# Four weight loads move from SyncE's queue to ScalarE's queue

## Chip, cores and metric

The kernel runs on one core of a Trainium2 chip. The metric is the device time of one launch in microseconds, the median of several runs. "Load" here means a DMA transfer from device memory (HBM) into SBUF; an engine's "queue" is the instruction stream from which a DMA is issued.

## What is computed

The reference chains three parts: attention with a window, a mixture of four experts that all tokens pass through, and a second mixture of eight experts in which each token is assigned to one.

```python
scores = scale * q @ k.T + bias            # B=2, H=8, S=768, D=64; 96 local keys and 8 global ones
a = softmax(where(keep, scores, -1e9));  x = (a @ v) as [1536, 512]
p = domain_probs / domain_probs.sum(-1)    # [1536, 4]
for e in range(4):
    x1 += p[:, e:e+1] * (relu(x @ w1[e]) @ w2[e])          # w1[e] 512x1024, w2[e] 1024x512
logits = x1 @ w_gate                       # greedy assignment by logit, 192 tokens for each of 8 experts
out[mask_e] = relu(x1[mask_e] @ v1[e]) @ v2[e]
```

## The kernel before

Every matrix product of the experts is done in float16 with a high and a low part, so that it keeps float32's accuracy. A weight matrix therefore goes through a small chain of its own before it can be used. One matrix (2 MB) is a *job* `k`; jobs 0 and 1 are the two matrices `w1[0]` and `w2[0]` of the first expert. Each job is loaded in two halves `f` of 1 MB, as 128 partitions of four rows of 2 KB. The steps are named as follows; a suffix `.k` is the job (none for job 0), and a digit the half or the quarter:

- `wl0`, `wl1` (`w_fetch`, L501 to L510; the DMA is on L507): the load of a half into a slot. The first four loads, `wl0`, `wl1`, `wl0.1`, `wl1.1`, go to two slots in the tile `y` and two in the tile `xT`. The next expert's loads, `wl0.2` to `wl1.3`, use the same four slots, and each waits for the lows that read the half before it.
- `wsq0`, `wsq1` (`w_norm`, L459): 16 small TensorE matmuls for each half that build a Gram matrix in PSUM, whose diagonal is the sum of squares.
- `wsum` (L463, L465): VectorE reads the Gram matrix against the identity (`gramj`), and one TensorE matmul adds over partitions. `wsc` (L330 to L335): VectorE makes a power of two from it, the scale `wsr`.
- `whi0` to `whi3` (L580 on ScalarE, L582 on GpSimd): the scaled high part of a quarter. `wlo0` to `wlo3` (L524): the low part, on VectorE, 1.3 us each.

The first phase interleaves these steps with the attention, which takes the 1536 rows as 12 tiles of 128. For a tile j: `load.j` and `loadv.j` (L592) load k, q and v; `sq` (L599, ScalarE) their squares; `total`, `scale` a power of two each; `hi`, `lo` (L580/L582, L648) their two parts; `T0`, `T1` the turned q and k (for tile 0 by TensorE and copies on ScalarE, L669, and VectorE, L667); `swap` a second turned q; `diag` a scaled identity; `qk`, `max`, `exp`, `ph`, `pl`, `PT`, `pv`, `x` the attention itself; `slope` prepares the bias (L386, L387). `gate` loads and squares the router's matrix.

The order in which all these steps are put into the program is written out by hand in the string `ORDER1`, and each engine runs its own instructions in that order. Its start, with the four loads in it, reads:

```python
    slope3 load sq1 sq0 gate0 loadv slope7 gate1 gate2 sq2 slope6 slope2 total wl0 scale hi1/G wsq0 hi0 hi2 lo0 slope4
    lo1 wl1 slope1 lo2 diag/A T0 T1 wsq1 wl0.1 slope0 wsum wsc swap wl1.1 qk0 whi3/G max0 qk1 load.1 whi0 max1 wsq0.1
    whi1/G wsq1.1 exp0 wlo3 wlo1 whi2 slope5 wsum.1 wlo0 loadv.1 ph0/G sq1.1 load.2 exp1 sq0.1 wlo2 wl0.2 sq2.1 wsc.1
```

All loads of this phase are issued by SyncE (SP). SP computes nothing, so that there a load's place in the order matters only against other DMAs. ScalarE computes `sq`, half of the `hi` steps, copies from PSUM and the exponentials.

Of the kernel before, what the change touches and what calls it, by code (L numbers as in the profile page):

```python
# [298 lines left out]
class Net:  # L299
# [201 lines left out]
    def w_fetch(s, k, f, slot):  # L501

        (m, e), i = s.jobs[k]
        w = s.w[m][i]
        src = w[e, :, 512 * f:512 * f + 512] if i == 0 else w[e, 512 * f:512 * f + 512, :]
        r = slot()
        s.nc.sync.dma_start(r, src.rearrange("(k p) f -> p k f", p=128))  # L507
        s.raws[k, f] = (r, None)
        s.when[k, f] = 0
        s.nload = max(s.nload, 2 * k + f + 1)  # L510
# [1371 lines left out]
```

## Time and profile before

| | us |
|---|---|
| median of 3 runs | 863.86 |
| lowest, highest | 862.59, 866.21 |
| the profiled execution's own time | 861.97 |
| its span from first to last instruction | 860.2 |
| TensorE busy (matmuls) | 777.3 (90%) |
| VectorE busy | 608.4 (71%) |
| ScalarE busy | 502.2 (58%) |
| GpSimd busy | 206.4 (24%) |

Busy time is a mean over stages that have different limits, so the rows below are of single stretches. In rows, PE is TensorE, PEld its weight loads, DVE VectorE, ACT ScalarE, POOL GpSimd, SP SyncE; a q behind a name (SPq, ACTq) is the engine's sequencer, which issues DMAs and semaphore instructions.

### The profile page before, as it was taken

How to read it: one execution, taken by the hardware profiler on the slowest of the kernel's cores; microseconds unless marked ns; L12 is line 12 of the kernel's file. 1: busy time of each engine (PE TensorE's matmuls, PEld its weight loads, DVE VectorE, ACT ScalarE, POOL GpSimd, SP SyncE). 2: the span in 40 equal slices, each digit the busy share in tenths (PEclk: the TensorE clock that was granted, in tenths of full speed). 3: DMA queues.
4: the chain of work that ended last, by engine and by line, in shares of the span. 5: the costliest groups of instructions: out<-in, count | busy, mean ns of one | idle time of the engine just before them, and what ended most of it. 6: DMA issues, size and time to landing. Idle time of an engine off the chain costs nothing. (4 is left out here: it accounts for less than half of the span.)

```text
span 860.2 us, 21736 instructions
## 1 busy us (share of the span) xinstructions
PE 777.3 (90%) x8916; PEld 600.1 (70%) x8920; DVE 608.4 (71%) x1467; ACT 502.2 (58%) x1004; POOL 206.4 (24%) x238
## 2 busy tenths in 40 slices
PE   3688999999999999999999999979998757999996
PEld 3477767777777767678888887534443357888996
DVE  5998888777763644547879999986674625797890
ACT  5887786745352323334557979631056417989852
POOL 3553352332442224240210112000000022222221
PEclk9689999999999999999999999989999869999999
DMA  8996769664447311691333320249014279899811
GB/s 272 265 191 140 130 154 171 120 136 88 99 73 207 104 51 51 125 178 31 75 71 69 77 59 26 63 103 330 34 32 140 76 237 332 253 265 335 174 38 38
DMA packets 219652, 116.38 MB, mean 135 GB/s; under 512 B 187424, under 2 KB 187424, under 8 KB 219552
## 3 DMA queue, kind: packets, MB, share of 16 engines
q1 hardware_dynamic: 217504, 108.64, 50.6%
q0 software_dynamic: 2048, 6.34, 3.1%
q8 instruction: 70, 1.15, 0.6%
q14 instruction: 30, 0.25, 0.1%
HBM read 69.30 MB, written 12.63 MB: 95 GB/s over the span
## 5 line engine op out<-in xcount | busy, mean ns | idle before, releaser
L886 PEld LDWEIGHTS <-w 128*128 128x128 f16 x3456 | 248.1, 98 | 37.9 <-issue 4.1
L886 PE MATMUL pH<-xT,w 128*128 128x128 f16 (+1 forms) x3168 | 252.9, 235 | 2.2 <-ACT H L860 1.6
L1072 PE MATMUL pY<-w,xT 128*128 128x512 f16 x384 | 120.7, 386 | 4.6 <-DVE y L1086 4.6
L897 PE MATMUL pY<-w,hh 128*128 128x512 f16 x384 | 114.7, 381 | 0.0
L1033 ACT ACTIVATE Cj<-C 128x256 bf16<-128x256 bf16 (+11 forms) x88 | 75.3, 855 | 28.2 <-DVE C L1024 21.6
L1305 PEld LDWEIGHTS <-w 128*128 128x128 f16 x768 | 66.4, 101 | 28.5 <-DMA xg<-g 16.2
L1072 PE MATMUL pY<-w,hl 128*128 128x512 f16 x192 | 74.1, 386 | 0.0
L897 PE MATMUL pY<-w,hl 128*128 128x512 f16 x192 | 73.1, 381 | 0.0
L860 ACT ACTIVATE H<-pH 128x512 f32<-128x512 f32 (+1 forms) x70 | 38.4, 554 | 55.1 <-PE pH L886 34.4
L1305 PE MATMUL pH<-xg,w 128*128 128x192 f16 x528 | 51.5, 259 | 19.5 <-DMA xg<-g 17.0
L1072 PEld LDWEIGHTS <-xT 128*128 128x128 f16 x384 | 36.5, 99 | 42.1 <-issue 8.6
L1325 PE MATMUL pR<-hh,w 128*128 128x192 f16 x512 | 64.9, 246 | 0.0
L1325 PEld LDWEIGHTS <-w 128*128 128x128 f16 x768 | 63.3, 98 | 2.0 <-issue 1.9
L1325 PE MATMUL pR<-hl,w 128*128 128x192 f16 x256 | 63.0, 246 | 0.0
L1022 DVE TENSOR_SCALAR C<-w,Lg 128x1024 bf16<-128x1024 f32 (+7 forms) x98 | 58.8, 615 | 0.6 <-PE pw L1039 0.4
L762 ACT ACTIVATE t<-pS,mx,ec 128x256 f32<-128x256 f32 (+1 forms) x96 | 51.6, 541 | 2.2
L777 POOL TENSOR_TENSOR pp<-t,pp 128x512 f16<-128x512 f32 (+1 forms) x34 | 40.1, 1183 | 44.4 <-ACT pp L580 35.9
L494 DVE SCALAR_TENSOR_TENSOR w<-w,wsr,w 128x1024 f16<-128x1024 f32 x32 | 40.4, 1279 | 10.0 <-ACT w L580 9.9
L584 DVE TENSOR_SCALAR hh<-H 128x384 f16<-128x384 f32 (+1 forms) x53 | 20.9, 396 | 37.5 <-ACT H L860 37.0
L897 PEld LDWEIGHTS <-hh 128*128 128x128 f16 x384 | 32.9, 98 | 19.6
L1452 POOL TENSOR_TENSOR hl<-H,hh 128x512 f16<-128x512 f32 x26 | 32.9, 1265 | 56.3 <-DVE hh L584 31.7
L469 ACT ACTIVATE junk<-w 128x2048 f16<-128x2048 f32 x16 | 30.5, 1906 | 25.4 <-DMA w<-in_moe_w_dram 25.4
(298 smaller groups left out, 1537.7 us busy)
## 6 DMA issues: line engine op xcount, KB each, us to landing
w<-in_moe_w_dram SPq DMA_DIRECT2D x16, 1024.0 KB, 13.0
raw<-in_moe_w_dram SPq DMA_DIRECT2D x16, 1024.0 KB, 7.8
hl<-in_moe_w_dram SPq DMA_DIRECT2D x8, 1024.0 KB, 5.5
y<-in_moe_w_dram SPq DMA_DIRECT2D x4, 1024.0 KB, 6.7
xT<-in_moe_w_dram SPq DMA_DIRECT2D x4, 1024.0 KB, 11.5
rows<-xs SPq DMA_DIRECT2D x12, 260.0 KB, 2.1
x<-in_k_dram SPq DMA_DIRECT2D x12, 256.0 KB, 3.3
x<-in_q_dram SPq DMA_DIRECT2D x12, 256.0 KB, 3.9
```

The source lines that it names most:

```text
L494: V.scalar_tensor_tensor(l, r[:, d2], sc, h, op0=OP.mult, op1=OP.subtract)
L762: s.nc.scalar.activation(t[:, hh], ps[:, hh], AF.Exp, bias=mx[:, 1, hh:hh + 1], scale=e[:, 0:1], accum_out=s.SU[j][:, 2 * g + hh:2 * g + h ...
L777: (G if eng == "G" else V).tensor_sub(pl[:, x], t, ph[:, x])
L860: s.nc.scalar.activation(H, ps, AF.Relu, scale=HS)
L886: nc.tensor.matmul(o[f], w[:, d, 128 * (f0 + f):128 * (f0 + f) + 128], x[:, :, c], start=(d == 0 and i == 0), stop=(d == 3 and i == 2))
L897: nc.tensor.matmul(py, l[:, f], w[:, f], start=(f == 0 and i == 0), stop=(f == 7 and i == 2))
L1022: V.tensor_scalar(C[:, 8 * i:8 * i + n], x[:, :n, e], l, None, op0=OP.is_ge)
L1033: s.nc.scalar.activation(x, C, AF.Copy, accum_out=s.AC[j][:, 1, e:e + 1])
L1072: nc.tensor.matmul(py, a[:, f], w[:, f], start=(n == 0), stop=(n == 23))
L1305: nc.tensor.matmul(ps[0][:, f % 2], w[:, d, 128 * f:128 * f + 128], xg[:, :, c], start=(k == 0), stop=(k == 11))
L1325: nc.tensor.matmul(ps[0][:, d % 2], w[:, f, 128 * d:128 * d + 128], h[:, f], start=(k == 0), stop=(k == 23))
L1452: (nc.gpsimd if eng == "G" else nc.vector).tensor_sub(x[1], P.pop((e, j, c)), x[0])
```

## The change

`w_fetch` issues the DMA on ScalarE's queue for jobs 0 and 1, and on SP's queue for all others as before. The place of the four steps in `ORDER1` stays, and so do their slots and sizes.

```diff
@@ -504,7 +504,7 @@
         w = s.w[m][i]
         src = w[e, :, 512 * f:512 * f + 512] if i == 0 else w[e, 512 * f:512 * f + 512, :]
         r = slot()
-        s.nc.sync.dma_start(r, src.rearrange("(k p) f -> p k f", p=128))
+        (s.nc.scalar if k < 2 else s.nc.sync).dma_start(r, src.rearrange("(k p) f -> p k f", p=128))
         s.raws[k, f] = (r, None)
         s.when[k, f] = 0
         s.nload = max(s.nload, 2 * k + f + 1)
```

## Rows read from the trace of the kernel before

**Rows 1.** Busy time by stretches: stretch, length, PE, PEld, DVE, ACT, POOL, clock, DMA share, GB/s

```profile
0.00:80.00 80.00, 53.10 (x677) 44.27 (x678) 67.29 (x170) 61.26 (x155) 36.50 (x45) 0.85 0.87 221
80.00:300.00 220.00, 216.09 (x2779) 163.12 (x2783) 155.42 (x337) 123.18 (x312) 74.50 (x78) 0.99 0.61 130
```

**Rows 2.** The same view, of two stretches of the start-up

```profile
16.00:24.00 8.00, 3.96 (x67) 3.15 (x64) 7.29 (x15) 6.73 (x18) 6.34 (x5) 0.99 0.85 205
...
24.00:40.00 16.00, 10.07 (x82) 8.02 (x83) 15.17 (x40) 13.51 (x33) 7.30 (x9) 0.50 0.96 264
```

**Rows 3.** The same view, of the first transfers

```profile
2.00:6.00 4.00, 0.00 (x0) 0.00 (x0) 2.18 (x11) 1.60 (x6) 1.11 (x4) 1.00 1.06 213
6.00:16.00 10.00, 4.51 (x49) 4.00 (x49) 4.65 (x13) 5.64 (x17) 2.10 (x4) 1.00 1.03 383
```

**Rows 4.** Timeline of SP's queue: start, duration of the issue, what

```profile
3.35 1.33 SPq L507 DMA_DIRECT2D y<-in_moe_w_dram  x2
4.72 1.50 SPq L507 DMA_DIRECT2D xT<-in_moe_w_dram  x2
...
8.25 7.32 SPq L592 DMA_DIRECT2D x<-in_q_dram  x1
...
23.53 1.88 SPq L507 DMA_DIRECT2D y<-in_moe_w_dram  x2
```

**Rows 5.** Timeline of TensorE: the Gram matmuls, with the idle time before

```profile
10.88 1.89 PE L459 MATMUL pY<-y 128*128 128x128 bf16 x16 [3.37 <-DMA y<-in_moe_w_dram]
...
15.16 1.09 PE L459 MATMUL pY<-y 128*128 128x128 bf16 x16
...
18.37 2.00 PE L459 MATMUL pY<-xT 128*128 128x128 bf16 x32
...
28.87 1.89 PE L459 MATMUL pY<-y 128*128 128x128 bf16 x16 [2.24 <-DMA y<-in_moe_w_dram]
```

**Rows 6.** Timeline of VectorE around the second job's Gram matrix

```profile
18.92 3.05 DVE L524 SCALAR_TENSOR_TENSOR w<-y,wsr,w 128x1024 f16<-128x1024 f32 x2
21.89 0.28 DVE L463 SCALAR_TENSOR_TENSOR gramj<-pY,ident 128x128 bf16<-128x128 f32 x1
```

**Rows 7.** Timeline of ScalarE, 6 to 25 us

```profile
6.59 0.61 ACT L599 ACTIVATE vs<-x 128x512 f16<-128x512 f32 x1
...
7.20 0.70 ACT L387 ACTIVATE bias<-y 128x256 bf16<-128x256 f32 x2
...
8.78 0.71 ACT L580 ACTIVATE vs<-x,asr 128x512 f16<-128x512 f32 x1
...
14.30 0.60 ACT L669 ACTIVATE kT<-pH 128x512 f16<-128x512 f32 x1 [0.47 <-PE pH L664]
...
17.19 0.60 ACT L669 ACTIVATE qT<-pH 128x512 f16<-128x512 f32 x1 [1.99 <-PE pH L664]
...
22.39 0.46 ACT L762 ACTIVATE t<-pS,mx,ec 128x128 f32<-128x128 f32 x1
...
24.02 0.63 ACT L599 ACTIVATE vs<-x 128x512 f16<-128x512 f32 x1
```

**Rows 8.** Instructions by line, ScalarE's sequencer: durations in ns, first to last start in us

```profile
L599 ACTq EVENT_SEMAPHORE  x1: 17/17/17, 22.4 to 22.4; - x1
...
L580 ACTq EVENT_SEMAPHORE  x1: 17/17/17, 17.2 to 17.2; - x1
```

**Rows 9.** Line L507: issues of the second pair, its landing, and eight later loads

```profile
L507 SPq DMA_DIRECT2D xT<-in_moe_w_dram x2: 507/730/953, 4.7 to 5.3; - x2
...
DMA to landing us min/median/max: 11.5/12.6/13.6
...
DMA to landing us min/median/max: 5.2/5.5/7.0
```

**Rows 10.** Waits of VectorE from 36 to 80 us: us, times, longest

```profile
DVE mx L754 <- PE pS L748: 0.6, 1, 0.6
...
DVE x L814 <- PE pO L802: 0.5, 1, 0.5
```

## The prediction

> **What bounds the kernel now.** I read the busy time by stretches first. From 80 to 300 us TensorE is busy 216.1 of 220 us, at a granted clock of 0.99 of the 2.4 GHz level; in the first 80 us it is busy only 53.1 [rows 1]. So the kernel is a TensorE-bound stream behind a start-up stage, and the change touches the start-up alone. All engines run an order written out by hand, so nothing that comes late can be overtaken on its own engine: a delay that reaches the engine that bounds the start-up comes out at the end, unless an idle gap absorbs it.
>
> Within the start-up the bound changes. From 16 to 24 us VectorE is busy 7.29 of 8 us and from 24 to 40 it is busy 15.17 of 16, with TensorE at 10.1 and at the lower clock (0.50, the 1.2 GHz level) [rows 2]. Before 16 us no engine is full; what the chain waits for is transfers. The DMA engines move 383 GB/s from 6 to 16 us, after 213 GB/s from 2 to 6, when the small-row loads of q, k and v run [rows 3]. The timeline of SP shows why: the four weight loads are issued from 3.35 to 6.2 us, right behind tile 0's q, k, v, and tile 1's k and q stand behind them (the issue of that q takes 7.32 us, from 8.25, so SP itself is held until about 15.6) [rows 4]. TensorE meets the first load at 10.88 after a wait of 3.37 us that DMA ended, the second at 15.16, and the last two together at 18.37, and is done with them at 20.37 [rows 5]. VectorE only comes to read that last result at 21.89, because two lows (`wlo3`, `wlo1`) keep it until 21.97 [rows 6]; so the loads of the second job have 1.5 us of slack there, and the first load has none.
>
> **The change, part by part.** *Removed from SP*: four issues, 2.83 us together (1.33 and 1.50) [rows 4]. SP's next entries, tile 1's k and q, move up to about 3.4 to 6 us; they also wait for tile 0's k and q to have landed. Nothing downstream waits for them now: their squares run from 21.4 us on, behind other ScalarE work. The entries after them wait for buffers that VectorE frees, as before. Gain on the path: 0. The transfers of tile 1's k and q (0.5 MB at 213 GB/s, an estimate of 2.5 us) now go ahead of the first weights, roughly from 5.6 to 8.1 us.
>
> *Added to ScalarE's queue*: four issues of 0.51 to 0.95 us, by the pair that SP issues from 4.7 us on [rows 9]. The trace has no DMA issued by ScalarE, so where in time they fall is the first unknown. In the hand order they stand behind these ScalarE instructions: `wl0` behind `sq2` and two slopes (6.59 and 7.20), `wl1` behind `hi2` (8.78), `wl0.1` behind the copy of kT (14.30), `wl1.1` behind the swap's copy of qT (17.19) [rows 7]. Two rows show how far ScalarE's sequencer is ahead of its engine. A semaphore instruction that belongs to the square at 24.02 ran at 22.4, just after the exponential at 22.39 had its wait met; four instructions lie between. Another, of the weight scaling that follows the swap's copy, ran at 17.2, as that copy got its operand [rows 8, 7]. So the sequencer passes everything whose waits are met and stands at the first whose wait is not. I take that for the issues: `wl0` at 6.6, `wl1` at 8.8, `wl0.1` at the start of the kT copy, `wl1.1` at the start of the swap's copy. The other end of the bound is that an issue waits for the end of the instruction ahead: `wl0` at 7.9 (7.20 + 0.70), the last two 0.6 us later. The first is nearer to the rows.
>
> *What the ScalarE issues hold up*: behind `wl0` stands `hi0`, which waits for VectorE until 8.15 anyway; the 0.5 to 0.95 us from 6.6 hide under `sq2` and the slopes. Behind `wl1` stand a slope and `diag`, not needed before 17 us. Behind `wl0.1` is a slope in an idle stretch. Behind `wl1.1` is the scaling `whi0`, next after that copy, which has half a microsecond of cover (the copy itself) and at worst loses 0.4 us, where the wait below is longer. Cost: 0.
>
> *How long a lone load takes*: the load of the next expert, issued at 23.53 into idle rings, ends TensorE's wait at 28.87: 5.3 us [rows 4, 5]. Eight loads of the same 1 MB later on took 5.2 at the least, 5.5 in the median [rows 9]. I take 5.3; the two loads of today in the crowded ring took 11.5 and 13.6 [rows 9], which is the far end and does not apply when each load goes out alone.
>
> *Step 1, the first load*: 6.6 + 5.3 = 11.9 instead of 10.88, +1.0 us. TensorE's in-order stream carries it through the transposes to both copies: the kT copy starts at 15.3, the swap's copy at 18.2.
>
> *Step 2, the second load*: issued at 8.8, its 2.7 us of data (1.05 MB at about 390 GB/s) come behind the first's and beside tile 1's v and tile 2's k and q, which SP now issues from about 10.4. It lands between 14.1 us (8.8 + 5.3) and 17.8 (behind all 0.79 MB of those three at 213 GB/s, 3.7 us more); it is wanted at 15.16 + 1.0 = 16.2. I take no wait, since two queues that share the engines will share them nearer to evenly than that; the bound is 1.6.
>
> *Step 3, the last two*: `wl0.1` issued at 15.3 lands at 20.6; `wl1.1` issued at 18.2 lands at 23.5. TensorE then needs 16 matmuls, 1.09 us (row at 15.16) to 1.89 us (rows at 10.88 and 28.87) [rows 5]: done at 24.6 to 25.4. VectorE reads the result 2.8 to 3.6 us later than 21.89. So the loss is not the first load's +1.0 but the last load's, which today is issued at 5.3 and would stand behind a copy that depends on the first load: the four loads become a chain.
>
> *Step 4, what is late next*: VectorE then does the two remaining lows, which free the buffers of the next expert's loads; SP issues those at 23.53 + 3.2, and the next wait of TensorE moves along. VectorE is nearly full until 40 us [rows 2], so nothing catches up there. From 36 to 80 us it waits three times for TensorE, 0.6 us the first and 0.5 each of the others [rows 10]; these waits hang on the same shifted streams, so I give nothing back; at most 1.6 us.
>
> *Sum*: + (2.8 to 3.6), middle 3.2 us, on the profiled execution's 861.97 us (span 860.2 and 1.8 around it): 865.2. That execution is 1.9 us below the median of the runs, so in terms of the median 863.86 + 3.2 = 867.1 us, +0.37%.
>
> A rule of the Trainium skill speaks against hoping for more bandwidth: "DMA: Bandwidth & Descriptors", section "Issuing engines are not separate DMA queues", says that loads from several issuing engines run on the same 16 DMA engines and that only issue time is saved. The row from 6 to 16 us agrees, since one queue alone already moves 383 GB/s; the sum above would be the same without it.
>
> **The rivals.** (a) *ScalarE issues only when the instruction ahead has ended*; the place is `wl0` at 7.9. The first load lands at 13.2 (+2.3), `wl1.1` goes out at 17.79 + 2.3 = 20.1, lands at 25.4, TensorE is done at 26.5 to 27.3: +4.7 to +5.5 us, 868.6 to 869.4, slower. For it: nothing shows a DMA overtaking compute on ScalarE. Against it: the two semaphore rows. It decides from an issue of `wl0` later than about 7.5. Chance 0.20.
>
> (b) *SP's and ScalarE's issues exclude each other.* SP's issue of a q load took 7.32 us while the ring was full [rows 4]; if the two issues of tile 1's k and q last until their data drain, 8.1 us by the estimate above, `wl0` can only start then and lands at 13.4: +2.5 in step 1, +4.7 us in all, 868.6. ScalarE's `hi0` would also slip by 0.7, hidden. Against it: the four weight loads went out back to back in 0.5 to 0.95 us each while earlier data was still moving. Chance 0.10. In the Trainium skill this is the lock on the shared descriptor generator in "Perfetto Trace Analysis", section "DMA Instruction — HWDGE (DVE, Sync)"; no run yet shows two queues at it.
>
> (c) *It is mostly hidden.* If a load into idle rings lands in about 4 us (2.7 us of data and little more), the first is there at 10.6, nothing shifts up to the swap's copy at 17.2, the last is there at 21.2 and done with at 22.3 to 23.1, so that VectorE waits only 0.4 to 1.2; or the gaps after 36 us give 1.6 back. Then 0 to +1.6: 863.9 to 865.5. Against it: no 1 MB load took under 5.2. Chance 0.15.
>
> (d) *Faster*: tile 1's inputs out from behind the weights would have to matter, with up to the 2.8 us that SP saves: 861.1. No wait on them stands in the timeline. Chance 0.05 for it and all else of that sign; even then it would stay within 0.5%.
>
> **How the numbers follow.** Forecast 0.50, (a) 0.20, (b) 0.10, (c) 0.15, (d) 0.05. About 0.5% (4.3 us) is what a measurement of this kernel can tell from no change. The likeliest case's own range is 866.7 to 869.1 (2.8, and 3.6 with the second load 1.6 late). The range to hold 8 in 10 reaches into (c) and (a): 863.5 to 870. Slower by over 0.5%: most of (a) and (b), 0.25, and 0.11 of the forecast, 0.36. Faster by over 0.5%: 0.03. Within: 0.61.
>
> **What would show it.** Right: ScalarE's issues at about 6.6, 8.8, 15.3 and 18.2; TensorE's first gram at 11.9; a wait for the last load until about 23.5; VectorE's read near 25; the same shift on the next expert's loads and where TensorE saturates. Wrong: an issue at 7.9 or stretched to several microseconds on ScalarE (a, b); the last load landing before 22 (c); a shift at 25 us that is gone by 80.

## The result and the profile after

The changed kernel takes 871.05 us (median of 5 runs, 869.59 to 871.72); the kernel before, run beside it on the same chip, takes 865.94 us (862.59 to 866.32). The ratio is 1.0072, with a 95% interval of 1.0045 to 1.0099: slower by 6.2 us (3.9 to 8.6; the medians themselves lie 5.1 us apart). The forecast was 867.1 us, a loss of 3.2, in a range of 863.5 to 870.0. The sign and the chain of loads came out as forecast; the loss is nearly twice as large, and the time lies 1.05 us above the range. That excess alone says little, since these runs of the kernel before lie 2.1 us above the 863.86 us from which the range was counted; the size of the loss is the firmer miss.

Read in the order of the prediction. Busy time by stretches of the changed kernel:

```profile
0.00:80.00 80.00, 49.75 (x603) 41.24 (x604) 62.12 (x160) 55.49 (x139) 35.07 (x44) 0.85 0.86 215
80.00:300.00 220.00, 214.03 (x2774) 162.29 (x2772) 160.74 (x346) 125.32 (x323) 75.14 (x77) 0.98 0.59 122
6.00:16.00 10.00, 3.07 (x26) 2.69 (x26) 3.36 (x12) 4.62 (x15) 2.10 (x4) 1.00 1.02 308
16.00:24.00 8.00, 6.09 (x69) 5.13 (x68) 5.02 (x12) 4.39 (x11) 3.35 (x4) 1.00 0.73 226
24.00:40.00 16.00, 7.03 (x61) 6.08 (x62) 12.55 (x25) 12.40 (x29) 6.59 (x8) 0.53 0.73 202
```

From 80 to 300 us TensorE is as busy as before (214.0 against 216.1 us [rows 1]); the difference is in the start-up. VectorE, the engine that had bounded it, falls from 7.29 to 5.02 us of the 8 from 16 on, and from 15.17 to 12.55 of the 16 from 24 on [rows 2]: it now waits.

The timeline of ScalarE, its four issues and the two copies from PSUM:

```profile
6.45 0.42 ACTq L507 DMA_DIRECT2D y<-in_moe_w_dram  x1
8.17 0.37 ACTq L507 DMA_DIRECT2D y<-in_moe_w_dram  x1
...
17.33 0.60 ACT L669 ACTIVATE kT<-pH 128x512 f16<-128x512 f32 x1 [1.20 <-PE pH L664]
17.34 0.37 ACTq L507 DMA_DIRECT2D xT<-in_moe_w_dram  x1
20.59 0.60 ACT L669 ACTIVATE qT<-pH 128x512 f16<-128x512 f32 x1 [2.36 <-PE pH L664]
20.60 0.37 ACTq L507 DMA_DIRECT2D xT<-in_moe_w_dram  x1
```

The third and the fourth load go out 0.01 us after the start of the copy they stand behind, not at its end: the sequencer had passed everything whose wait was met. The copies themselves come 3.0 and 3.4 us later than before (14.30 and 17.19 [rows 7]). From issue to landing, line L507, the first pair (6.4 to 8.2 us) and the second:

```profile
L507 ACTq DMA_DIRECT2D y<-in_moe_w_dram x2: 374/397/420, 6.4 to 8.2; - x2
...
DMA to landing us min/median/max: 6.7/7.2/7.8
...
L507 ACTq DMA_DIRECT2D xT<-in_moe_w_dram x2: 374/374/374, 17.3 to 20.6; - x2
...
DMA to landing us min/median/max: 5.3/5.3/5.4
```

The lone loads of the second pair take the 5.3 us of the forecast; the very first one takes 6.7. The timeline of TensorE:

```profile
13.18 1.89 PE L459 MATMUL pY<-y 128*128 128x128 bf16 x16 [5.66 <-DMA y<-in_moe_w_dram]
...
17.51 1.91 PE L459 MATMUL pY<-y 128*128 128x128 bf16 x16
19.91 1.07 PE L664 MATMUL pH<-identh,qn 128*64 128x128 f16 x16
22.69 1.09 PE L459 MATMUL pY<-xT 128*128 128x128 bf16 x16 [0.59 <-DMA xT<-in_moe_w_dram]
26.02 1.89 PE L459 MATMUL pY<-xT 128*128 128x128 bf16 x16 [2.24 <-DMA xT<-in_moe_w_dram]
34.69 1.89 PE L459 MATMUL pY<-y 128*128 128x128 bf16 x16 [2.42 <-DMA y<-in_moe_w_dram]
```

Two things are to be seen. The waits for DMA are now in front of the first, the third and the fourth half (5.66, 0.59, 2.24 us), where before only the first half was waited for (3.37 [rows 5]). And the second group of 16 Gram matmuls takes 1.91 us, where it took 1.09 [rows 5]. The same 16 matmuls take 1.89 us where the clock column reads 0.50 [rows 2, 5], the 1.2 GHz level, so 1.09 is the 2.4 GHz level: the rise of the clock now comes after that group. (The column reads 1.00 from the start up to its first fall, also over the first group, which takes 1.89; for the first 20 us only the durations tell.) Last, VectorE:

```profile
22.48 2.68 DVE L524 SCALAR_TENSOR_TENSOR w<-y,wsr,w 128x1024 f16<-128x1024 f32 x2
27.95 0.29 DVE L463 SCALAR_TENSOR_TENSOR gramj<-pY,ident 128x128 bf16<-128x128 f32 x1 [2.80 <-PE pY L459]
```

Its read of the second Gram matrix is at 27.95 instead of 21.89 [rows 6], +6.06 us, with an idle time of 2.80 us before it. Matched one to one, VectorE's 1467 instructions show how that goes on: +7.6 at 100 us, +8.0 at 400, +6.6 at 680, +9.8 at the end. The profiled execution of before (861.97 us) lies 4.0 us below the median of before in this comparison, so the later figures run above the ratio's 6.2. The delay isn't given back.

### The profile page after: what moved, and what is told of

It is laid out like the page before. It is cut to its first block, busy times and chain, and to the rows that moved or that the text cites. A ratio compares the mean times of both kernels' runs of the same rounds, so it can differ in the third digit from the quotient of the medians.

```text
span 869.9 us, 21739 instructions
## 1 busy us (share of the span) xinstructions
PE 778.5 (89%) x8920; PEld 602.1 (69%) x8920; DVE 610.5 (70%) x1467; ACT 502.0 (58%) x1004; POOL 206.1 (24%) x238
```

## The experiments

All times are ratios to runs of the kernel before on the same chip, given here in us of its median (862 us). "Read" is the start of VectorE's read of the second Gram matrix against 21.89; the shifts at 100 and at 400 us are of VectorE's matched instructions against the trace of before. Read and shifts compare one execution with one, while the runs of one kernel lie up to 9 us apart; the whole time is from all runs.

```
                                         read    at 100  at 400   whole time, 95%
the change                               +6.06    +7.6    +8.0    +6.2 (3.9 to 8.6)
A only the second job on ScalarE         +5.5     +5.4    +3.6    +6.6 (4.0 to 9.2)
B only the first job on ScalarE          +5.9     +4.4    +4.6    +5.2 (3.2 to 7.2)
C all four first in the order            +8.4     +9.4    +7.8    +9.6 (7.1 to 12.0)
D change, last two moved up              +3.5     +3.6    +3.7    +3.4 (1.6 to 5.1)
E change, all four early                 +2.0     +1.0    +0.3    +1.5 (-0.3 to 3.2)
F change, first Gram behind T0, T1       +4.5     +5.1    +4.9    +5.3 (3.2 to 7.4)
G before, first Gram behind T0, T1       -0.1     -1.0    -0.8    -0.5 (-2.3 to 1.3)
H change + 64 warm-up matmuls            +5.7     +9.0    +4.4    +6.3 (4.1 to 8.4)
I D + 48 warm-up matmuls                 +1.5     +3.1    -1.4    -2.8 (-4.1 to -1.4)
J E + 24 warm-up matmuls                 -0.3     -0.3    -3.3    -2.8 (-4.2 to -1.4)
K before + 30 warm-up matmuls            -1.9     -2.5    -6.0    -6.3 (-8.5 to -4.1)
L before + 1 matmul, buffers swapped     +1.3     +0.7    +0.6    -0.1 (-2.2 to 2.0)
M before + 30, buffers not swapped       -0.9     +1.4    -2.9    -5.7 (-7.8 to -3.4)
N D + 48, buffers not swapped            +1.9     +2.4    -1.8    -4.2 (-6.3 to -2.2)
O change + 48, buffers not swapped       +5.5     +6.8    +2.1    -1.3 (-3.1 to 0.4)
```

**A, B: half of the change.** Which pair of loads carries the loss?

```diff
-        (s.nc.scalar if k < 2 else s.nc.sync).dma_start(r, ...)
+        (s.nc.scalar if k == 1 else s.nc.sync).dma_start(r, ...)     # A
+        (s.nc.scalar if k == 0 else s.nc.sync).dma_start(r, ...)     # B
```

> Only the second pair (wl0.1, wl1.1) is issued by ScalarE, at its old place in the order; the first pair stays on SP. Theory of the chain (each load is late by the place of its issue, and the last one stands behind copies that hang on the first): the first load lands as before at 10.9 us, the last is issued at 17.2 and lands at 22.6, VectorE reads the second Gram matrix 1.8 to 2.6 us later than before, and the whole kernel is slower by 1.8 to 2.6 us. Rival, the first load alone is what costs: nothing moves, 0 to 0.5 us. Rival, an issue on ScalarE costs by itself: about half of the change's 6 us.

> Only the first pair (wl0, wl1) is issued by ScalarE; the second pair stays on SP and so goes out ahead of it. Theory of the chain: the first load lands at 13 to 14.5 us (behind or beside the second pair), both copies start 3 to 4 us late, nothing waits for the second pair any more, and VectorE reads the second Gram matrix 3 to 4 us late: slower by 3 to 4 us. If the last load's lateness were all of the loss: 1.0 us or less.

Both halves lose nearly all of it, each in its own way, and more than was expected (1.8 to 2.6 and 3 to 4 us). In A the first load is there as before, but the last two are issued at 14.65 and 18.75, behind the copies, and take 6.5 and 6.7 us; the last group starts at 25.45. Part of that is not the chain's. TensorE in A:

```profile
11.02 1.89 PE L459 MATMUL pY<-y 128*128 128x128 bf16 x16 [3.39 <-DMA y<-in_moe_w_dram]
...
15.67 1.92 PE L459 MATMUL pY<-y 128*128 128x128 bf16 x16
```

After the same first wait as in the kernel before (3.37 us [rows 5]) the second group runs at the lower clock all the same, and the swap's copy comes 1.6 us late (18.75). In B the second pair goes out ahead of the first, and the first Gram group starts at 17.09 instead of 10.88. So the two losses don't add up: either alone brings the read to +5.5 or +5.9.

**C: all four loads first in the order**, still on ScalarE's queue.

```diff
-    slope3 load sq1 sq0 ... total wl0 scale ... lo1 wl1 slope1 ... wsq1 wl0.1 slope0 wsum wsc swap wl1.1 qk0
+    wl0 wl1 wl0.1 wl1.1 slope3 load sq1 sq0 ... total scale ... lo1 slope1 ... wsq1 slope0 wsum wsc swap qk0
```

> All four loads are issued by ScalarE as in the change, but stand at the very start of the order, ahead of ScalarE's first bias step, so that they go out at 0.7 to 3 us. Theory of the place in the queue: the first load lands at or before 10.9 us, no later chain arises, and the kernel is back within 2 us of the one before, on either side. Rival, the queue itself (two rings, or issues that hold ScalarE up) is what costs: slower by about 6 us as in the change.

It lost 9.6 us, and the theory, that only the place behind compute costs, fell for this extreme. The timeline, ScalarE and then VectorE:

```profile
0.73 1.18 ACTq L507 DMA_DIRECT2D y<-in_moe_w_dram  x2
1.94 4.96 ACTq L507 DMA_DIRECT2D xT<-in_moe_w_dram  x2
...
12.58 0.63 ACT L599 ACTIVATE vs<-x 128x512 f16<-128x512 f32 x1 [3.33 <-DMA x<-in_q_dram]
...
17.64 0.16 DVE L330 TENSOR_SCALAR ase<-pq 128x3 int32<-128x3 int32 x1 [13.29 <-PE pq L606]
```

The weights are there by 6.8 and 9.8 us and nobody can use them: tile 0's q lands at 12.5, the router's small matrix and v later still, and the scale that everything waits for runs at 17.64 instead of 7.55. From 7 to 11 us the trace counts 166 to 171 transfers of 2 KB (weights) and 169 to 183 of 256 B (q, k, v) in each us: the two queues get nearly equal numbers, so the 256 B rows get a ninth of the bytes. In the Trainium skill, "DMA: Bandwidth & Descriptors", section "Queues, rings and completion order", each DMA engine takes turns, packet by packet, between the queues that have work for it. The equal counts agree with such turns; how many transfers a turn takes, the trace doesn't show.

**D: the chain taken apart.** The last two loads directly behind the second.

```diff
-    lo1 wl1 slope1 lo2 diag/A T0 T1 wsq1 wl0.1 slope0 wsum wsc swap wl1.1 qk0
+    lo1 wl1 wl0.1 wl1.1 slope1 lo2 diag/A T0 T1 wsq1 slope0 wsum wsc swap qk0
```

> The change, with the second pair's two loads moved up in the order to stand right behind wl1, ahead of the copies that hang on the first load; all four still on ScalarE. Theory of the chain (the loss is the last load, which waits for a copy that waits for the first load): ScalarE issues all four by 10 us, the last lands by about 21, TensorE does not wait for it, and VectorE reads the second Gram matrix when its own lows are done, about 3.2 us later than before instead of 6.1: half of the change's loss comes back. Rival, the first load's lateness sets the end: nothing comes back.

Half of the loss is gone. The timeline, ScalarE, TensorE, VectorE:

```profile
9.14 0.59 ACTq L507 DMA_DIRECT2D xT<-in_moe_w_dram  x1
...
20.82 0.60 ACT L669 ACTIVATE qT<-pH 128x512 f16<-128x512 f32 x1 [2.36 <-PE pH L664]
...
22.42 2.20 PE L459 MATMUL pY<-xT 128*128 128x128 bf16 x32
...
25.40 0.28 DVE L463 SCALAR_TENSOR_TENSOR gramj<-pY,ident 128x128 bf16<-128x128 f32 x1
```

The last two halves run as one group of 32 with no wait in front of them, and VectorE reads without idle time. What is left, 3.5 us, is the first load's lateness (TensorE starts at 13.42) and the lower clock behind it (I, below): the swap's copy comes as late as in the changed kernel.

**E: early, but behind tile 0's first input.** The four loads stand between the squares.

```diff
-    slope3 load sq1 sq0 gate0 loadv slope7 gate1 gate2 sq2 slope6 slope2 total wl0 scale
+    slope3 load wl0 sq1 wl1 sq0 wl0.1 gate0 loadv slope7 gate1 gate2 wl1.1 sq2 slope6 slope2 total scale
-    lo1 wl1 slope1 ... wsq1 wl0.1 slope0 wsum wsc swap wl1.1 qk0
+    lo1 slope1 ... wsq1 slope0 wsum wsc swap qk0
```

> All four loads on ScalarE, but spread between tile 0's first squares, so that they go out between 4.4 and 6.6 us, when tile 0's k, q and v are mostly in. Theory of the place: the first load lands at 10.5 to 11.5 us, the last by 19, no wait behind it, and the kernel is within 1.5 us of the one before. Rival, ScalarE's queue as such costs: slower by 5 us or more, as the change and the variant with the four loads at the very start.

The issues go out from 4.39 to 6.13 us, about a microsecond later than SP's of before [rows 4], the first Gram group starts at 11.69, and the loss is 1.5 us (-0.3 to 3.2), no longer told from zero. So most of the change's loss is the place in the queue, and not the queue as such. The queue isn't free, though. ScalarE in E:

```profile
5.63 2.68 ACTq L507 DMA_DIRECT2D xT<-in_moe_w_dram  x2
...
8.42 0.63 ACT L599 ACTIVATE vs<-x 128x512 f16<-128x512 f32 x1 [1.55 <-issue]
```

The last of the four issues alone took 2.18 us (from 6.13), and the square behind it starts at 8.42 instead of 6.59 [rows 7], so that the scale of tile 0 is made at 9.39 instead of 7.55. Here TensorE was waiting for the first load until 11.69 anyway, which hides it.

**F, G: the first Gram group behind the transposes.** TensorE no longer waits for the first load before T0 and T1.

```diff
-    ... hi1/G wsq0 hi0 hi2 ... diag/A T0 T1 wsq1
+    ... hi1/G hi0 hi2 ... diag/A T0 T1 wsq0 wsq1
```

> The change, with TensorE's first Gram matmuls moved behind the transposes of tile 0, so that the kT copy no longer hangs on the first load. Theory of the chain: the kT copy starts at 11 to 12 us and the third load is issued there instead of at 17.3; the swap's copy, which still hangs on the first two loads, starts at 18 to 19.5, the last load lands 5.3 to 7 us later, and VectorE reads the second Gram matrix 3 to 5 us late instead of 6.1. Rival, no link there: as the change.

> The kernel before (all loads on SP) with the same move of the first Gram matmuls behind the transposes. The start-up chain before has its first load at 10.9 us on the path; with the transposes done in that wait, the second Gram comes up to 1.5 us earlier if its load has landed (13.6), and the kernel is 0 to 1.5 us faster. If VectorE's work alone sets the start-up, nothing moves.

With it the kT copy is at 12.71 and the third load leaves at 12.72, 4.6 us earlier than in the changed kernel; but the fourth still waits for the swap's copy at 18.71, and the read comes at +4.5. One link of the chain is worth 1.5 us at the read, and the same move in the kernel before changes nothing there (-0.1), so the gain is the chain's and not the move's. In the whole time 5.3 us (3.2 to 7.4) can't be told from the change's 6.2.

**H to K: the clock.** Extra matmuls ahead of the first Gram group keep TensorE busy while it waits for the first load.

```diff
+            if k == 0 and q == 0:
+                heat = s.pY.tile([128, 512], F32, name="pY")[:, 0:128]
+                for i in range(64):          # H; 48 in I, 24 in J, 30 in K
+                    nc.tensor.matmul(heat, s.ones, s.ones, start=True, stop=True)
             if q == 0:
                 J["gram"] = s.pY.tile([128, 512], F32, name="pY")[:, 0:128]
```

> The change, and 64 more TensorE matmuls of 128x128 on constants just ahead of the first Gram matmuls, in the wait for the first load; their result is not used. Theory of the clock (after the longer wait TensorE's granted clock rises to the 2.4 GHz level only at 21.6 us, instead of 13.6, and the second Gram, the transposes and the swap run at half speed): the clock is up by 13 us, the second Gram takes 1.1 us instead of 1.9, the swap's copy starts 0.9 to 1.2 us earlier than in the change, and so does VectorE's read of the second Gram; 0.9 to 1.5 us of the change's 6 come back. Rival, the clock is no matter: the same as the change.

> The changed kernel with the last two loads placed right behind the second (as in the run that takes the chain apart, which lost 3.4 us) and with 48 more TensorE matmuls ahead of the first Gram matmuls; their result is not used. Theory that the lower granted clock over the second Gram, the transposes and the swap is a part of the loss by itself: the clock rises near 13 to 14 us instead of 22.9, the swap's copy starts near 18.7 instead of 20.8, and with the loads not chained to it the last one is there at 22.2 as before, so VectorE reads the second Gram matrix at 23.4 to 24.2 (+1.5 to +2.3 us against 21.89) and the total is 1.5 to 2.3 us over the kernel before. Rival, that the clock there only shows that TensorE waits and costs nothing: the read stays at 25.4 and the total at +3.4 us.

> The four loads on ScalarE's queue in the early places of the run that lost 1.5 us (between tile 0's squares), with 24 more TensorE matmuls ahead of the first Gram matmuls; their result is not used. Theory that what is left of the loss with early places is the granted clock, which there rose only at 20.0 us: the clock rises by 14 us, VectorE reads the second Gram matrix at 22.0 to 22.8 and the total is within 0.8 us of the kernel before. Rival, that the rest comes from the landing of the loads: the read stays near 23.9 and the total near +1.5 us.

> The kernel before with 30 more TensorE matmuls ahead of the first Gram matmuls, inside its first wait; their result is not used. VectorE sets the time of the read of the second Gram matrix there (TensorE is done 1.5 us earlier), so the theory expects the read at 21.9 and the total within 0.8 us of the kernel before. Rival, that the clock before 13.6 us costs the kernel before as well: the read 0.8 us or more earlier, and the total 1 us lower.

In I and J the clock theory holds at the read. TensorE and VectorE in I:

```profile
16.22 1.09 PE L463 MATMUL pY<-y 128*128 128x128 bf16 x16
...
23.39 0.29 DVE L467 SCALAR_TENSOR_TENSOR gramj<-pY,ident 128x128 bf16<-128x128 f32 x1 [0.34 <-PE pY L463]
```

The second Gram group takes 1.09 us, the swap's copy comes earlier, and the read is at 23.39 against 25.40 in D; in J it is at 21.64 against 23.90 in E: 2.0 and 2.3 us that the lower level had cost. In H the swap's copy is 2.0 us earlier than in the changed kernel (18.59), but the last load takes 7.0 us instead of 5.4 and eats it: the read gains 0.4 us, the whole time nothing. K was expected to change nothing, and that was wrong: the read in the kernel before also moves, from 21.89 to 19.96, because the first Gram matrix and what VectorE makes of it come earlier. And the whole times of I, J and K lie 4.3, 2.5 and 4.4 us below what their reads explain (I was expected 1.5 to 2.3 us over the kernel before, J level with it); in the table the shift falls by 3.0 to 4.5 us between 100 and 400 us. The extra tile also swaps the two buffers of the pool pY for the rest of the program, which could have been that cause.

**L to O: the buffers told from the clock.** L takes the extra tile with a single matmul; M, N and O spread the warm-up over two tiles, so that all later ones lie as before.

```diff
+            for h in range(2 if (k, q) == (0, 0) else 0):     # M, N, O
+                heat = s.pY.tile([128, 512], F32, name="pY")[:, 0:128]
+                for i in range(15):                           # 24 in N and O
+                    nc.tensor.matmul(heat, s.ones, s.ones, start=True, stop=True)
```

> The kernel before with one more buffer of the two-buffer PSUM pool pY taken ahead of the first Gram matrix, and a single matmul into it, whose result is not used. So nothing is warmed, but from there on every tile of that pool lies in the other of its two buffers, as in the runs with warm-up matmuls. Theory that the 3.5 to 6 us that those runs gained between 90 and 400 us come from the swapped buffers: VectorE's read of the second Gram matrix stays at 21.9 us, and the shift of VectorE's instructions goes from 0 before 90 us to -3 to -4.5 at 400 us; the total is 3 to 4 us lower. Rival, that they come from the warm-up: no shift anywhere beyond 1 us, the total as the kernel before.

> The kernel before with 30 warm-up matmuls ahead of the first Gram matmuls as in the earlier run, but in two halves that take one pY buffer each, so that all later tiles lie in the same buffers as in the kernel before; the results are not used. By the theory of the swapped buffers only the direct gain is left: the read at about 20.0 us (-1.9), -1 to -2 us up to 400 us, total 1 to 2 us lower. By the rival, that the warm-up itself gave all of it: -5 to -6 us at 400 us and 6 us in all again.

> The changed kernel with its last two loads behind the second (chain taken apart) and 48 warm-up matmuls, now over two pY buffers, so that later tiles lie as in the kernel before; their results are not used. If the granted clock at the start costs what the read shows (25.40 without the warm-up, 23.4 with it), the read is at 23.4 again and the total 1.2 to 2.3 us over the kernel before. If what the earlier run won was all warm-up, the total is again 2.5 to 3.5 us under it.

> The changed kernel, order untouched, with 48 warm-up matmuls over two pY buffers; their results are not used. Clock theory: kT copy and swap's copy 1.5 to 2 us earlier than in the changed kernel (15.5 and 18.5), the last load issued at about 18.5; with a landing of 5.4 us as in the changed kernel it is there at 24 and the read at 25.5 (+3.6), the total +3 to +4 us; with a landing of 7 us, as in the earlier run with warm-up, there is no gain over the changed kernel, the read at 27.6 and the total +5 to +6.5. Rival, that the clock is only a sign of waiting: the swap's copy at 20.6 as in the changed kernel.

The theory of the swapped buffers fell: L gains nothing, M gains 5.7 us, as K does. The warm-up gives it. O, the changed kernel with nothing but the warm-up, is level with the kernel before (-1.3 us, -3.1 to 0.4), although its read is still at +5.5 and +3 us or more was expected. H, with 64 matmuls, is the exception: it ends no earlier than the changed kernel, though its shift at 400 us is 3.6 us smaller; why is open. The timelines of TensorE and VectorE in M:

```profile
11.54 1.09 PE L463 MATMUL pY<-y 128*128 128x128 bf16 x16 [0.26 <-DMA y<-in_moe_w_dram]
...
20.98 0.28 DVE L467 SCALAR_TENSOR_TENSOR gramj<-pY,ident 128x128 bf16<-128x128 f32 x1
```

Its read is 0.9 us earlier, but nothing of that is left at 100 us (+1.4); at 400 us M is 2.9 us ahead, and the rest of the 5.7 comes later still. One place in between can be shown. Busy time by stretches around 384 us in the kernel before:

```profile
380.00:384.00 4.00, 3.18 (x33) 2.54 (x34) 2.17 (x6) 1.24 (x3) 2.88 (x3) 0.78 0.88 172
384.00:388.00 4.00, 4.00 (x73) 3.43 (x71) 1.05 (x6) 0.60 (x1) 1.01 (x2) 0.79 1.00 213
```

and in M:

```profile
380.00:384.00 4.00, 3.63 (x47) 3.14 (x45) 2.05 (x10) 1.95 (x4) 3.30 (x4) 1.00 0.95 187
384.00:388.00 4.00, 4.00 (x74) 3.60 (x73) 1.78 (x7) 0.47 (x1) 0.00 (x0) 1.00 0.78 168
```

The column before the DMA share is the granted clock: a short fall in the kernel before (0.78, 0.79) that M doesn't have. Eight of the ten kernels without warm-up have that fall between 381 and 394 us, the seven with warm-up have none. But A and C have none either, without any warm-up. The same view of A:

```profile
384.00:388.00 4.00, 2.06 (x32) 1.87 (x32) 2.98 (x8) 0.97 (x3) 2.07 (x2) 1.00 1.38 172
388.00:392.00 4.00, 4.00 (x81) 3.64 (x79) 1.62 (x9) 0.87 (x2) 1.83 (x2) 1.00 0.95 202
```

So the warm-up isn't needed to be without it. From 380 to 390 us the matched instructions of M gain 1.8 us, and those of A 1.5; M gains two smaller steps of 0.5 and 0.9 us behind 281 and 359 us, where in the kernel before TensorE waits 0.42 us for ScalarE and 0.72 us for a DMA, and in M it doesn't. Why twenty matmuls and more at 8 us change waits at 281, and what decides on the clock at 384, isn't settled.

## Why the prediction was wrong in size

*Removed from SP, gain 0: right.* SP's next entries moved up (tile 1's k at 3.37, q at 4.17), and nothing came earlier for it.

*ScalarE's sequencer runs ahead: right.* 6.6, 8.8 and "at the start of the copies" were predicted; 6.45, 8.17, 17.34 and 20.60 with copies at 17.33 and 20.59 were found. That falsifies rival (a), which needed `wl0` at 7.9, and (b): SP's two issues of tile 1's k and q took 0.76 and 0.82 us, and ScalarE's four 0.37 to 0.42. Rival (a)'s price of 4.7 to 5.5 us came nearer to the result than the forecast, for a reason that isn't in it.

*ScalarE held up, 0, and step 2, no wait for the second load: right.* The scaling behind the swap's copy starts 0.49 us after it, as before. The second load is there at 15.9 us and the group that reads it follows without a wait (17.51).

*Step 1, the first load lands 5.3 us after its issue: too small.* This is the first term that failed. It took 6.7 us, so the first Gram group starts at 13.18 and not at 11.9: +1.3. A load has landed when the parts of all 16 DMA engines are in. Here 15 were there by 11.41, 5.0 us after the issue, so the 256 B transfers that still ran until 7.8 us didn't slow the load as a whole; the last part came 1.7 us later. This is no chance of one trace: in D, F, I, N and O, with the same place of issue, 14 or 15 parts are there by 11.54 and the last at 12.84 to 13.47. Only in H, issued at 7.00, do all 16 come by 11.97. Why a part lags is open. The eight later loads took 5.2 to 7.0 us [rows 9], but the prediction put 5.3 into its sum and the 7.0 into no bound.

*Carrying it to the copies by a constant shift: wrong, and this is the term that was left out.* The prediction added +1.0 to 14.30 and 17.19. From the start of the first Gram group to the swap's copy, 6.31 us in the kernel before (10.88 to 17.19), it is 7.41 now: the second group takes 1.91 instead of 1.09 and the transposes of the swap 1.07 instead of 0.64, since the clock rises only behind them (the trace's first record of the 2.4 GHz level is at 21.6 us, at 13.6 before). That is +1.1: 0.8 up to the transposes, 0.2 in them. I and J confirm its kind by taking it back (2.0 and 2.3 us at the read). In the changed kernel itself the warm-up brings the swap's copy 2.0 and 2.2 us forward (H, O) and the read only 0.4 and 0.6, because the last load then takes 7.0 us; so the terms of the sum below depend on each other. That the longer first wait delays the rise isn't shown: in A and L the first group runs at its old time (11.02, 10.91) and the second still takes 1.92 us, in L with the read 1.3 us late. Of the kernels without warm-up only before and B have that group at 1.1 us, so the early rise in the one trace of before may be chance, and how much of the loss this term is in other executions stays open.

*Step 3, the chain of loads: right.* `wl1.1` leaves with the swap's copy, takes 5.4 us, and the wait for it is the last. D takes the chain apart and gets 2.6 of 6.06 us back at the read, 2.8 of 6.2 in the time. The 16 matmuls behind it took 1.89 us, the upper end of the bound, +0.4 against the middle.

*The sum at the read*, so corrected: 3.2 + 1.3 + 1.1 + 0.4 = 6.0, measured 6.06. (The forecast's own terms, 18.2 + 5.3 + 1.09 to 1.89 less 21.89, give 2.7 to 3.5, 0.1 less than it states.)

*Step 4, no give-back: right.* In the kernels without warm-up the shift of the read and the whole time agree within their intervals (5.5 and 6.6, 5.9 and 5.2, 8.4 and 9.6, 3.5 and 3.4, 2.0 and 1.5, 4.5 and 5.3). The trace of before has a fourth wait for TensorE from 36 to 80 us, of 0.2 us, that the bound left out. Rivals (c) and (d) are out: no 1 MB load in any trace took under 4.8 us, where (c) needed about 4, and nothing gained.

Further theories of mine fell on the way: that early issues can hardly hurt (C), that K would change nothing, and the swapped buffers (L). The totals expected of A, B, H, I, J and O were missed as well.

Before with the warm-up (K 856.63, M 857.65 us against 862.72 and 861.64) is faster than the kernel before by 0.73% (0.48 to 0.99) and 0.66% (0.40 to 0.91), and so than the changed one. It keeps the loads on SP's queue. With the warm-up the unchained loads on ScalarE's queue (N, 0.9951) and the early ones (J, 0.9968) also beat the kernel before, but by no more than K or M.

## What to carry to other kernels

In these runs a DMA issued from ScalarE's queue left when that queue's sequencer got to it, once the last unmet wait ahead of it was met. Put a load there only ahead of compute that doesn't itself wait for that load or one before it, or the loads become a chain at a full landing time (here 5.3 to 6.7 us) each; and look at how long the issue itself may last, since ScalarE stands still behind it (E). When a load comes late, don't carry TensorE's work behind it along by a constant shift: look at how long that work takes at either level of the clock. And earlier isn't always better: in C the large-row loads took eight ninths of the bytes while small-row ones ran beside them.

## What the runs showed of the hardware

- ScalarE's sequencer issues a DMA while the engine ahead of it is still computing: 0.01 us after the start of a 0.60 us copy, twice.
- 1 MB loads on ScalarE's queue landed 5.0 to 7.8 us after their issue when at most one other weight load was under way (the change, A, F, H). The first load's last part came 1.3 to 2.2 us behind most of the others in six of seven runs.
- An issue on ScalarE's queue took 0.37 to 0.42 us in the change and up to 2.18 us in E, where the next instruction of ScalarE started only behind it.
- Two queues at work got nearly equal numbers of transfers: about 170 a microsecond each, of 2 KB in one and 256 B in the other (C).
- 30 matmuls in an idle wait of TensorE at 7 to 11 us made the kernel before 6 us faster (K, M). The read at 22 us is 0.9 to 1.9 us earlier; between 100 and 400 us 3.5 to 4.3 us are gained, 1.5 to 1.8 of them from 380 to 390 us, where the kernel before has a fall of the granted clock that these lack. A and C lack it without a warm-up; what links the two is open.
